# State products moved behind the outputs' products, and PReLU given to two engines in turn: a Mamba-2 scan with a two-layer PReLU network behind it

## The chip, the cores and the metric

The kernel runs on one core of one Trainium2 chip. The metric is the time of one execution on the device in microseconds. A core has TensorE (PE: matrix products, which write to the accumulation memory PSUM), VectorE (DVE), ScalarE (ACT), GpSimd (POOL) and SyncE (SP), which in this kernel issues nearly all transfers. Each engine works through its own queue in order, and engines wait for each other through semaphores.

## The reference

Everything is fp32. A state-space scan over 4 batches, 8 heads, 768 positions in chunks of 32 (the result does not depend on the chunk), head size 32, state size 16; its output is laid out as 3072 tokens of 256 features and goes through two matrix products with a PReLU between them.

```python
for c in range(nc):                       # chunks of one (batch, head)
    cum = np.cumsum(la, axis=-1)          # la = log(clip(a, 1e-6, 1))
    L = np.exp(cum[:, :, :, None] - cum[:, :, None, :]) * causal
    y_intra = np.einsum('bhij,bhjd->bhid', CB * L, xc)        # CB = C B^T
    y_inter = np.einsum('bhin,bhnd->bhid', Cc, state) * np.exp(cum)[..., None]
    state = decay_full * state + sum_j(B_j x_j * decay_from_j)
...
x = attn_out.transpose(0, 2, 1, 3).reshape(3072, 256)
h = x @ w_in                              # 256 x 2048
g = np.maximum(h, 0.0) + alpha * np.minimum(h, 0.0)
return g @ w_out                          # 2048 x 256
```

## The kernel before

**Pairs.** The scan uses chunks of 128 positions, two chunks (a *pair*) at a time: 12 pairs, three to a batch. `pair(gp)` is a generator: each `yield` ends a stage, and `ssm(gp, n)` runs the next n stages of a pair. The stages of a pair from 4 on (`fine`) are: transposes of B and C (L469) and a copy to `bc` by ScalarE (L472); four pieces of the decays by VectorE (`half_decays`, two scans each, L438), with the spread of C by ScalarE (`spread_c`, L484) at the last; the *state products* (`added`, L520: what the pair adds to the state, from x and `bn`, two chunks, or one for the pair that closes a batch), the state update (`states`, L532 by VectorE or L529 by ScalarE at a batch's first pair; the masked `sm` by GpSimd, L535) and the decayed C (`c_decayed`, GpSimd, L487); the products of B and C (`products_bc`, L570, four row groups, of which the first two go to PSUM tiles of `ss_tile()` and the last two to `spare()`) and two of the four multiplications by the decays (L606); the other two; the *outputs' products* (L622 from the state, L629 within the chunk) and the copies of their two tiles to `xT` by ScalarE (L636). `pair_loads` makes `bn` on GpSimd (L385) from the loaded B. From `early[0] = None` on (L1002), `ss_tile()` hands out two PSUM tiles in turn.

**Groups and quads.** Two pairs make a group of 512 tokens. Group 0 goes through the network by `hidden` and `output`, while the weights arrive in 16 pieces, which are converted by `convert_a` (ScalarE and GpSimd, L218 to L228) and `convert_b`/`convert` (VectorE and GpSimd). The loop over `f` (L978) runs this stage; tile f of the hidden layer gets its PReLU at L651 (ScalarE) and L652 (VectorE). The decay rows of the second two batches are loaded at f = 5 (L122, on SP's queue) and prepared by VectorE at f = 8 (L339). Groups 1 to 5 use a form with seven products instead of eight (a Strassen-Winograd scheme), in four *quads* each (z = 0 to 3, `quad(g, z, after)`): seven first-layer products, two PSUM tiles A and Y (both of the `hp` ring of two, which `spare()` shares), PReLUs, sums by GpSimd (L806, L815), and then seven second-layer products (`product`, L747), which the next quad issues between its own. The first-layer products come in the order: A; Y; A again; A with the third token sum; Y with b22; A with the fourth token sum; Y with b21. Between them ScalarE copies A out (L780, L789), VectorE adds (L791, L795), and, ahead of the last product, ScalarE copies the saved first product into Y (L801). `combine` adds up the finished group's second-layer products during the next group's first quad, with ScalarE copies at L831 and L834.

**The order of the work** is written out by hand (`manual_schedule`): every engine executes its instructions in the order in which the program issues them. `quad` calls `after(j)` for j = 1 to 14, and `after` issues there what belongs to step j: a second-layer product of the quad before (`with_gram` in quads with z even while there is a pair to come, `without` otherwise; the first has nothing at step 9), weight sums, and stages of the pairs (`steps`: which pair's next stage runs at (z, j)). A group's two pairs belong to the next group: one is worked on from z = 3 of the group before to z = 1, the other from z = 1 to z = 3. The state products stand at (0, 9) and (2, 9), between the products A with the fourth token sum and Y with b21; the outputs' products at (1, 5) and (3, 5).

**PReLU** in a quad (`prelu`, L751) is, for a tile of two halves p, o = h * (alpha * s) by ScalarE and then o = max(h * s, o) by VectorE: one operation per half, first both of ScalarE (L755), then both of VectorE (L757). Both read h from the same PSUM tile, save for the one called g22, whose h is in SBUF (`c22`).

Of the kernel before, what the change touches and what calls it, by code (L numbers as in the profile page):

```python
# [9 lines left out]
F32 = mybir.dt.float32  # L10
U32 = mybir.dt.uint32
U16 = mybir.dt.uint16
ALU = mybir.AluOpType
# [9 lines left out]
def kernel(  # L23
# [25 lines left out]
    nc = tc.nc  # L49
# [6 lines left out]
    P = 128  # L56
    Q = 128
# [268 lines left out]
    held = {}  # L326
    bns = {}

    def identity_bank():


        m5_bank.append(bank(3))
        nc.scalar.copy(out=m5_bank[0][:, HT:], in_=ident_h[:, :HT])
        ident_p.append(m5_bank[0][:, HT:])
# [77 lines left out]
    def spare():  # L412

        return ps_h.tile([P, GT], F32, name="hp", tag="hp")

    def pair(gp):

        b, c = divmod(2 * gp, CPB)
        nat, abc, xt, ap = loads["p", gp]
        last = c + 2 == CPB  # L420
        dec = work.tile([P, 2, H, Q], F32, name="dec")
        dv = dec.rearrange("p k h t -> p k (h t)")

# [37 lines left out]
            yield  # L461


        tp = spare() if gp == 1 else ss_tile()
        if gp == 0:
            keep_warm(tp, 3, Q)
# [23 lines left out]
        fine = gp >= 2 * GC // 2  # L490
        if gp < 2:
            spread_c()
        if gp == 0:
# [2 lines left out]
            dps = spare()  # L496
            keep_warm(dps, 6, Q)
            yield
        bn = bns.pop(gp) if gp in bns else pair_loads(gp)
        if gp == 1:  # L500
            c_decayed()
            dps = spare()
# [1 line left out]
        elif gp:  # L504
            yield

        nk = 1 if last else 2  # L510
        st = [masked.get(b)]
        new = work.tile([P, 2, P], F32, name="state")
        sm = work.tile([P, 2, P], F32, name="sm")

        def added(dps):
            dps = dps.rearrange("p (k m) -> p k m", m=P)
            for k in range(nk):
                for w in range(KC):
                    ws = slice(64 * w, 64 * w + 64)
                    nc.tensor.matmul(dps[ws, k], bn[:, k, ws], xt[:, k, w * P : (w + 1) * P],  # L520
                                     start=True, stop=True, tile_position=(0, 64 * w),
                                     skip_group_check=True)
            return dps

        def states(dps):
            for k in range(nk):
                old = state.get(b)
                if old is None:
                    nc.scalar.copy(out=new[:, k], in_=dps[:, k])  # L529
                else:  # L530
                    e = (k + 1) * Q - 1
                    nc.vector.scalar_tensor_tensor(out=new[:, k], in0=old, scalar=pf[:, e : e + 1],  # L532
                                                   in1=dps[:, k], op0=ALU.mult, op1=ALU.add)
                state[b] = new[:, k]
            nc.gpsimd.tensor_tensor(out=sm[:, :nk], in0=new[:, :nk],  # L535
                                    in1=hmask.unsqueeze(1).to_broadcast([P, nk, P]), op=ALU.mult)
            st.extend(sm[:, k] for k in range(nk))
            masked[b] = st[-1]

        if fine:  # L540
            for k in range(2):
                for w in range(2):
                    half_decays(k, w)
                    if k == 1 and w == 1:
                        spread_c()
                    yield
        else:
            if gp > 1:
                states(added(ss_tile()))
                c_decayed()  # L550
# [33 lines left out]
        if gp == 0:  # L584
            gram = products_bc()
            dps = added(dps)
            yield
            c_decayed()
            times(dec[:, :, :2], one_less(gram))
        elif gp == 1:  # L590
            gram = products_bc()
            g0 = one_less(gram)
            yield
            decays(1)
            states(dps)
            times(dec[:, :, :2], g0)
        else:
            if fine:
                states(added(ss_tile()))
                c_decayed()  # L600
            yield
            gram = products_bc()
        for i, r in enumerate(r for r in ((2, 3, 0, 1) if fine else (3, 2, 1, 0) if gp > 1 else range(4))
                              if r in gram):
# [6 lines left out]
        yield  # L611


        y = [ss_tile()[:, : 2 * Q].rearrange("p (k t) -> p k t", k=2) for w in range(KC)]
        if gp < 2:
            keep_warm(y[0].rearrange("p k t -> p (k t)"), 2 - gp)
        begun = False
# [7 lines left out]
        for k in range(2):  # L625
            for w in range(KC):
                for q in range(4):
                    h = 4 * w + q
                    nc.tensor.matmul(y[w][32 * q : 32 * q + 32, k], xt[:, k, h * D : (h + 1) * D],  # L629
                                     dec[:, k, h], start=False, stop=True,  # L630
                                     tile_position=(0, 32 * q), skip_group_check=True)
        g, q = divmod(2 * gp, GC)
        if q == 0:
            xts[g] = xtp.tile([P, KC, GT], F32, name="xT")
# [116 lines left out]
    def prelu(o, h, z, i, by=(nc.scalar, nc.vector)):  # L751

        fs = [slice(4 * z + 2 * p + i, 4 * z + 2 * p + i + 1) for p in range(2)]
        for p in range(2 if nc.scalar in by else 0):
            nc.scalar.mul(o[:, p], h[:, p], s_alpha[:, fs[p]])  # L755
        for p in range(2 if nc.vector in by else 0):
            nc.vector.scalar_tensor_tensor(out=o[:, p], in0=h[:, p], scalar=s_mul[:, fs[p]],  # L757
                                           in1=o[:, p], op0=ALU.mult, op1=ALU.max)

    def quad(g, z, after):  # L760

# [261 lines left out]
    for i in range(NZ * (NG - 1)):  # L1023
        g, z = divmod(NZ + i, NZ)
        nxt = 2 * g + 2

        def after(j, g=g, z=z, i=i, nxt=nxt):
            places = with_gram if nxt < NP and z % 2 == 0 else without
            if i and j in places:
                product(*divmod(NZ + i - 1, NZ), places[j])  # L1030
            if i == 0:
                for f, half in last_out.get(j, ()):
                    output(NF - LATE + f, half)
            if (i, j) in ((0, 13), (1, 2)):
# [24 lines left out]
        quad(g, z, after)  # L1059
# [31 lines left out]
```

## Time and profile before

| what | value |
|---|---|
| median of 10 runs | 374.3 us (373.64 to 374.84) |
| the profiled execution: time, span | 374.0 us, 372.1 us |
| TensorE clock granted | 0.999 |
| busy: PE, DVE, POOL, ACT | 98%, 65%, 54%, 48% of the span |
| L747 products (second layer), 128x256 | 320 and 240 records, 381 and 379 ns each |
| L772 products (first layer), 128x256 | 480 records in three groups, 379 to 390 ns each |
| L757 PReLU by VectorE | 120 on PSUM, 479 ns each |
| L755 PReLU by ScalarE | 120 on PSUM, 470 ns each |
| L815 sums by GpSimd | 58, 1269 ns each |

How to read it: the span is the stretch from the first to the last instruction in the profile, and what lies around it makes the difference to the execution's time. An fp32 product appears as two records, so that one `first` (two products) is four. A record's duration is longer than the distance to the next one, since products are pipelined: 379 ns against 216 ns from start to start. The timeline merges neighbouring instructions of a kind; its columns are the start in microseconds from the span's start, the length of the merged stretch in microseconds, the engine, the line, the operation, output <- input by the program's names, for TensorE the rows and columns of the array in use, the shape, and the count; in square brackets stands the idle time before it and what ended it. Idle time of an engine that is not the bottleneck costs nothing by itself.

### The profile page before, as it was taken

What the parts mean: (1) busy time and instruction counts of PE and PEld (TensorE: products, weight loads), DVE (VectorE), ACT (ScalarE), POOL (GpSimd) and SP (SyncE); (2) the same over time, 40 slices, a digit from 0 to 9 for tenths busy, and PEclk for the clock granted to TensorE, in tenths of its full rate; (3) what the DMA queues carried; (4) which work ended last, traced back from release to release, by engine and by line L of the source; (5) the groups of instructions that cost most, each with busy time, mean ns of one, the idle gap of its engine ahead of it and who ended that gap; (6) DMA issues with size and microseconds to landing.
All of it is one profiled execution on the core that took longest, in us unless ns stands there. A gap on an engine that the chain in (4) does not pass through costs nothing.

```text
span 372.1 us, 6183 instructions
## 1 busy us (share of the span) xinstructions
PE 365.0 (98%) x2223; PEld 294.5 (79%) x2223; DVE 243.3 (65%) x462; ACT 179.4 (48%) x384; POOL 200.7 (54%) x211
## 2 busy tenths in 40 slices
PE   8989999999999999999999999999999999999996
PEld 8766656578788888788788788788788788888884
DVE  7996889976448548748638847637848644643364
ACT  2657866435355355445444445445535525553541
POOL 4875566777929654724644625555445355264512
PEclk9999999999999999999999999999999999999999
DMA  8989998902176201005504603701901001001004
GB/s 162 201 171 342 220 289 187 194 11 58 56 129 113 71 3 56 2 0 78 136 3 66 146 2 56 158 0 31 176 8 29 2 0 25 7 0 30 1 0 85
DMA packets 121878, 30.71 MB, mean 83 GB/s; under 512 B 93736, under 2 KB 117752, under 8 KB 121848
## 3 DMA queue, kind: packets, MB, share of 16 engines
q1 hardware_dynamic: 116736, 29.74, 35.7%
q10 hardware_dynamic: 5112, 0.59, 1.1%
q8 instruction: 17, 0.28, 0.3%
q14 instruction: 13, 0.11, 0.1%
HBM read 26.98 MB, written 3.34 MB: 81 GB/s over the span
## 4 chain that ended last, share of the span: by engine, by line
PE 87%; DMA 5%; DVE 4%; SPq 2%; ACTq 1%; ACT 1%; issue 1%; POOL 0%; POOLq 0%; DVEq 0%
PE hp L772 34%; PE bank L747 32%; PE bank L686 6%; PE hp L648 4%; DMA raw<-in_moe_w_in_dram 3%; PE ss L629 3%; PE ss L570 2%; PE ss L622 1%; DVE dec L438 1%; PE ss L520 1%; DMA nat<-in_B_dram 1%; PE hp L570 1%; PE ss L469 1%; SPq L165 1%; DMA ap<-pf 1%; SPq L163 1%
## 5 line engine op out<-in xcount | busy, mean ns | idle before, releaser
L815 POOL TENSOR_TENSOR gt<-gt 128x512 f32<-128x512 f32 x58 | 73.6, 1269 | 30.7 <-DVE gt L757 23.8
L757 DVE SCALAR_TENSOR_TENSOR gt<-hp,s_mul,gt 128x256 f32<-128x256 f32 x120 | 52.5, 479 | 46.8 <-ACT gt L755 45.8
L747 PE MATMUL bank<-gt,w_out 128*128 128x256 f32 x320 | 82.4, 381 | 0.0
L755 ACT ACTIVATE gt<-hp,s_alpha 128x256 f32<-128x256 f32 x120 | 50.3, 470 | 46.7 <-PE hp L772 32.5
L747 PEld LDWEIGHTS bank<-gt,w_out 128*128 128x128 f32 x320 | 60.1, 190 | 10.4 <-issue 2.3
L806 POOL TENSOR_TENSOR gt<-gt 128x512 f32<-128x512 f32 x20 | 25.4, 1271 | 78.8 <-DVE gt L757 78.8
L747 PE MATMUL bank<-gt,ws 128*128 128x256 f32 x240 | 58.3, 379 | 0.0
L747 PEld LDWEIGHTS bank<-gt,ws 128*128 128x128 f32 x240 | 45.1, 190 | 5.8
L438 DVE TENSOR_TENSOR_SCAN dec<-abc,bank 128x256 f32<-128x256 f32 x80 | 48.1, 661 | 0.0
L772 PE MATMUL hp<-xs,w_in 128*128 128x256 f32 x160 | 42.8, 390 | 0.0
L772 PE MATMUL hp<-xT,w_in 128*128 128x256 f32 x160 | 41.9, 384 | 0.0
L772 PE MATMUL hp<-xs,ws 128*128 128x256 f32 x160 | 41.1, 379 | 0.0
L791 DVE TENSOR_TENSOR hp<-hp,u 128x512 f32<-128x512 f32 x20 | 14.0, 700 | 39.8 <-ACT u L789 39.8
L780 ACT COPY m<-hp 128x512 f32<-128x512 f32 x20 | 11.7, 586 | 51.8 <-PE hp L772 51.8
L772 PEld LDWEIGHTS hp<-xs,w_in 128*128 128x128 f32 x160 | 28.7, 189 | 7.7 <-issue 3.0
L772 PEld LDWEIGHTS hp<-xs,ws 128*128 128x128 f32 x160 | 30.4, 190 | 4.1
L772 PEld LDWEIGHTS hp<-xT,w_in 128*128 128x128 f32 x160 | 29.7, 190 | 5.0 <-issue 1.4
L686 PE MATMUL bank<-w_out,gt 128*128 128x256 f32 x128 | 31.0, 384 | 0.0
L686 PEld LDWEIGHTS bank<-w_out,gt 128*128 128x128 f32 x128 | 23.7, 190 | 6.6 <-issue 3.5
L795 DVE TENSOR_TENSOR c<-hp,m 128x512 f32<-128x512 f32 x20 | 13.6, 681 | 19.3 <-PE hp L772 19.3
L648 PE MATMUL hp<-xT,w_in 128*128 128x512 f32 x48 | 22.8, 598 | 0.9 <-DVE gt L652 0.7
L789 ACT COPY u<-hp 128x512 f32<-128x512 f32 x20 | 11.7, 585 | 22.5 <-PE hp L772 22.5
(156 smaller groups left out, 553.3 us busy)
## 6 DMA issues: line engine op xcount, KB each, us to landing
abc<-z SPq DMA_DIRECT2D x20, 512.0 KB, 5.2
raw<-in_moe_w_in_dram SPq DMA_DIRECT2D x8, 512.0 KB, 5.0
raw<-in_moe_w_out_dram SPq DMA_DIRECT2D x8, 512.0 KB, 7.3
xt<-in_x_dram SPq DMA_DIRECT2D x24, 128.0 KB, 2.8
out_dram<-o_sb SPq DMA_DIRECT2D x32, 64.0 KB, 1.9
nat<-in_B_dram SPq DMA_DIRECT2D x22, 64.0 KB, 2.8
nat<-in_C_dram SPq DMA_DIRECT2D x22, 64.0 KB, 2.6
ap<-pf SPq DMA_DIRECT2D x11, 128.0 KB
```

The lines of the kernel that those rows point to most:

```text
L438: nc.vector.tensor_tensor_scan(out=dv[:, k, hs], data0=abc[k][:, hs], data1=ident_p[0], initial=0.0, op0=ALU.mult, op1=ALU.add)
L648: nc.tensor.matmul(hp, w_in[:, k, f * P : (f + 1) * P], xts[g][:, k], start=(k == 0), stop=(k == KC - 1))
L686: nc.tensor.matmul(pos[0][t // 2][:, t % 2], gt[:, t * Q : (t + 1) * Q], w_out[:, f], start=(f == 0 and t % 2 == 0), stop=(f == NF - 1), s ...
L747: nc.tensor.matmul(ms[g][i][:, h], w, blocks[g, z][n][:, p], start=(q == 0 and h == 0), stop=(q == NQ - 1), skip_group_check=True)
L755: nc.scalar.mul(o[:, p], h[:, p], s_alpha[:, fs[p]])
L757: nc.vector.scalar_tensor_tensor(out=o[:, p], in0=h[:, p], scalar=s_mul[:, fs[p]], in1=o[:, p], op0=ALU.mult, op1=ALU.max)
L772: nc.tensor.matmul(to[:, p], w(2 * z + p), b, start=start and p == 0, stop=True, skip_group_check=True)
L780: nc.scalar.copy(out=m1, in_=A)
L791: nc.vector.tensor_tensor(out=Y, in0=Y, in1=u2, op=ALU.add)
L795: nc.vector.tensor_tensor(out=c22, in0=A, in1=m5, op=ALU.add)
L806: nc.gpsimd.tensor_tensor(out=tc_, in0=g22, in1=g12, op=ALU.subtract)
L815: eng.tensor_tensor(out=o, in0=x0, in1=x1, op=ALU.subtract)
```

## The change

It has four parts. (1) `prelu` goes through the two halves and issues ScalarE's operation and VectorE's for the first half, and then both for the second. (2) A fine pair's generator is reordered: `bn` and the state products come first, then the state update, then transposes, decays and the rest; `c_decayed` joins `spread_c`. The state products of the next pair are written into the unused second half of the outputs' second PSUM tile (`beside`), and a `yield` stands between the outputs' products and the copies to `xT`. At (1, 5) and (3, 5) the loop now issues: the outputs' products, the next pair's state products, the two copies to `xT`, and the next pair's state update. The stages at (0, 9) and (2, 9) are gone; `bn` is made there. (3) Pair 4 runs its first four stages ahead of the loop over quads (state products and update among them), with `bn` made at f = 14. (4) The first part of the conversion of weight piece 6 is issued at f = 5, behind the sixth tile's (f = 5) PReLU by ScalarE, instead of at the end of f = 4. Moved code is shown shortened:

```diff
+    beside = {}
...
         def added(dps):
-            dps = dps.rearrange("p (k m) -> p k m", m=P)
+            dps = dps[:, : 2 * Q].rearrange("p (k m) -> p k m", m=P)
...
         if fine:
+            bn = bns.pop(gp) if gp in bns else pair_loads(gp)
+            dps = added(beside.pop(gp) if gp in beside else ss_tile()[:, : 2 * Q])
+            yield
+            states(dps)
+            yield
...
         if fine:
             for k in range(2):
                 for w in range(2):
                     half_decays(k, w)
                     if k == 1 and w == 1:
                         spread_c()
+                        c_decayed()
                     yield
...
         else:
-            if fine:
-                states(added(ss_tile()))
-                c_decayed()
-            yield
+            if not fine:
+                yield
             gram = products_bc()
...
-        y = [ss_tile()[:, : 2 * Q].rearrange("p (k t) -> p k t", k=2) for w in range(KC)]
+        ys = [ss_tile() for w in range(KC)]
+        y = [t[:, : 2 * Q].rearrange("p (k t) -> p k t", k=2) for t in ys]
+        if fine:
+            beside[gp + 1] = ys[1][:, 2 * Q :]
...
+        if fine:
+            yield
         g, q = divmod(2 * gp, GC)
...
     def prelu(o, h, z, i, by=(nc.scalar, nc.vector)):
...
-        for p in range(2 if nc.scalar in by else 0):
-            nc.scalar.mul(o[:, p], h[:, p], s_alpha[:, fs[p]])
-        for p in range(2 if nc.vector in by else 0):
-            nc.vector.scalar_tensor_tensor(out=o[:, p], in0=h[:, p], scalar=s_mul[:, fs[p]],
-                                           in1=o[:, p], op0=ALU.mult, op1=ALU.max)
+        for p in range(2):
+            if nc.scalar in by:
+                nc.scalar.mul(o[:, p], h[:, p], s_alpha[:, fs[p]])
+            if nc.vector in by:
+                nc.vector.scalar_tensor_tensor(out=o[:, p], in0=h[:, p], scalar=s_mul[:, fs[p]],
+                                               in1=o[:, p], op0=ALU.mult, op1=ALU.max)
...
-        if f < FIRST + 2:
-            convert_a(*pieces[f + 1 + (f > FIRST)])
+        for i in {FIRST: (5,), FIRST + 1: (6, 7)}.get(f, ()):
+            convert_a(*pieces[i])
         convert_next(first=f > FIRST)
-        if f == FIRST:
-            convert_a(*pieces[6])
+        if f == 14:
+            bns[4] = pair_loads(4)
...
-    ssm(2 * GC // 2, 2)
+    ssm(2 * GC // 2, 4)
...
-    steps = {(0, 1): 0, (0, 2): 0, (0, 5): 0, (0, 9): 0, (0, 13): 0, (1, 1): 0, (1, 5): 0,
-             (1, 12): 1, (1, 14): 1, (2, 1): 1, (2, 2): 1, (2, 5): 1, (2, 9): 1, (2, 13): 1,
+    steps = {(0, 1): 0, (0, 2): 0, (0, 5): 0, (0, 13): 0, (1, 1): 0, (1, 5): 0,
+             (1, 12): 1, (1, 14): 1, (2, 1): 1, (2, 2): 1, (2, 5): 1, (2, 13): 1,
              (3, 1): 1, (3, 5): 1, (3, 12): 2, (3, 14): 2}
...
                 ssm(nxt + steps[z, j])
+
+                if j == 5 and z % 2:
+                    for p in (1, 0, 1):
+                        if nxt + z // 2 + p < NP:
+                            ssm(nxt + z // 2 + p)
...
-            ahead = nxt + {(1, 3): 1, (3, 8): 2}.get((z, j), NP)
+            ahead = nxt + {(0, 9): 1, (2, 9): 2}.get((z, j), NP)
```

More of the change, by code (lines that the diff above doesn't have):

```diff
@@ L420, in pair @@
         last = c + 2 == CPB
+        fine = gp >= 2 * GC // 2
         dec = work.tile([P, 2, H, Q], F32, name="dec")
@@ L461, in pair, with added, states @@
             yield
+        nk = 1 if last else 2
+        st = [masked.get(b)]
+        new = work.tile([P, 2, P], F32, name="state")
+        sm = work.tile([P, 2, P], F32, name="sm")
+        def added(dps):
+            dps = dps[:, : 2 * Q].rearrange("p (k m) -> p k m", m=P)
+            for k in range(nk):
+                for w in range(KC):
+                    ws = slice(64 * w, 64 * w + 64)
+                    nc.tensor.matmul(dps[ws, k], bn[:, k, ws], xt[:, k, w * P : (w + 1) * P],
+                                     start=True, stop=True, tile_position=(0, 64 * w),
+                                     skip_group_check=True)
+            return dps
+        def states(dps):
+            for k in range(nk):
+                old = state.get(b)
+                if old is None:
+                    nc.scalar.copy(out=new[:, k], in_=dps[:, k])
+                else:
+                    e = (k + 1) * Q - 1
+                    nc.vector.scalar_tensor_tensor(out=new[:, k], in0=old, scalar=pf[:, e : e + 1],
+                                                   in1=dps[:, k], op0=ALU.mult, op1=ALU.add)
+                state[b] = new[:, k]
+            nc.gpsimd.tensor_tensor(out=sm[:, :nk], in0=new[:, :nk],
+                                    in1=hmask.unsqueeze(1).to_broadcast([P, nk, P]), op=ALU.mult)
+            st.extend(sm[:, k] for k in range(nk))
+            masked[b] = st[-1]
+        if fine:
[4 more added lines that the diff above has]
+            yield
         tp = spare() if gp == 1 else ss_tile()
@@ L488, in c_decayed @@
                                     op=ALU.mult)
-        fine = gp >= 2 * GC // 2
         if gp < 2:
@@ L498, in pair @@
             yield
-        bn = bns.pop(gp) if gp in bns else pair_loads(gp)
+        if not fine:
+            bn = bns.pop(gp) if gp in bns else pair_loads(gp)
         if gp == 1:
@@ L505, in pair @@
             yield
[L510 to L515, printed above, removed]
-            dps = dps.rearrange("p (k m) -> p k m", m=P)
[L517 to L538, printed above, removed]
         if fine:
@@ L597, in pair @@
         else:
-            if fine:
-                states(added(ss_tile()))
-                c_decayed()
-            yield
+            if not fine:
+                yield
             gram = products_bc()
@@ L631, in pair @@
                                      tile_position=(0, 32 * q), skip_group_check=True)
+        if fine:
+            yield
         g, q = divmod(2 * gp, GC)
```

## The prediction

> **What bounds the kernel now.** I read the page first, then the chain of waits, then the timeline of TensorE, ScalarE and VectorE in one stretch of the main loop, then the list of who waited for whom.
>
> ```profile
> PE 365.0 (98%) x2223; PEld 294.5 (79%) x2223; DVE 243.3 (65%) x462; ACT 179.4 (48%) x384; POOL 200.7 (54%) x211
> PE   8989999999999999999999999999999999999996
> PE 87%; DMA 5%; DVE 4%; SPq 2%; ACTq 1%; ACT 1%; issue 1%; POOL 0%; POOLq 0%; DVEq 0%
> ```
>
> TensorE is busy in every slice and carries 87% of the chain that ended last; nobody else holds more than 5%. So a change counts in two ways only: what TensorE itself does, and whether it now has to wait. The reader should see that the second is a matter of slack on ScalarE and VectorE, whose low shares say nothing about latency. The TensorE timeline of an even quad (z = 2) with a pair in hand:
>
> ```profile
> 177.23 1.03 PE L772 MATMUL hp<-xs,w_in 128*128 128x256 f32 x4
> 178.19 0.66 PE L520 MATMUL ss<-xt,bn 128*64 128x128 f32 x8
> 178.78 1.13 PE L772 MATMUL hp<-xT,w_in 128*128 128x256 f32 x4
> 179.74 1.03 PE L747 MATMUL bank<-gt,w_out 128*128 128x256 f32 x4
> ...
> 181.58 0.71 PE L570 MATMUL hp<-cz,bc 32*128 32x256 f32 x2
> ...
> 183.83 1.03 PE L772 MATMUL hp<-xT,w_in 128*128 128x256 f32 x4
> ```
>
> One product of four records takes 0.863 us start to start (0.216 each). From 177.23 to the product of 179.74 pass 2.51 us, where two products alone would take 1.73: the state products (L520) cost 0.78 us, of which 0.09 on entering and 0.10 on leaving (the record after them lasts longer, 1.13 against 1.03). The two engines beside it:
>
> ```profile
> 175.75 0.84 ACT L755 ACTIVATE gt<-hp,s_alpha 128x256 f32<-128x256 f32 x2 [1.33 <-PE hp L772]
> 176.48 0.90 ACT L755 ACTIVATE gt<-c,s_alpha 128x256 f32<-128x256 f32 x2
> 177.59 0.59 ACT L801 COPY hp<-m 128x512 f32<-128x512 f32 x1 [0.21 <-DVE gt L757]
> 178.36 0.84 ACT L755 ACTIVATE gt<-hp,s_alpha 128x256 f32<-128x256 f32 x2 [0.17 <-PE hp L772]
> 180.00 0.84 ACT L755 ACTIVATE gt<-hp,s_alpha 128x256 f32<-128x256 f32 x2 [0.81 <-PE hp L772]
> ```
>
> ```profile
> 175.43 0.67 DVE L795 TENSOR_TENSOR c<-hp,m 128x512 f32<-128x512 f32 x1
> 176.63 0.88 DVE L757 SCALAR_TENSOR_TENSOR gt<-hp,s_mul,gt 128x256 f32<-128x256 f32 x2 [0.53 <-ACT gt L755]
> 177.42 0.87 DVE L757 SCALAR_TENSOR_TENSOR gt<-c,s_mul,gt 128x256 f32<-128x256 f32 x2
> 179.23 0.88 DVE L757 SCALAR_TENSOR_TENSOR gt<-hp,s_mul,gt 128x256 f32<-128x256 f32 x2 [0.94 <-ACT gt L755]
> 180.02 0.72 DVE L532 SCALAR_TENSOR_TENSOR state<-state,ap,ss 128x128 f32<-128x128 f32 x2
> 180.88 0.88 DVE L757 SCALAR_TENSOR_TENSOR gt<-hp,s_mul,gt 128x256 f32<-128x256 f32 x2
> ```
>
> Two things to see. A PReLU out of PSUM is two ScalarE operations and then two VectorE ones, never mixed: VectorE starts at 176.63, 0.04 after ScalarE's second ends (0.04 to 0.09 over the twenty quads). And the copy L801 ends at 178.18, while the product that adds into the same tile starts at 178.78: 0.6 us of slack, made by the state products that stand in between.
>
> **What the Trainium skill says.** "PSUM — Partial Sum Buffer", section "PSUM bank collisions raise a hardware error": two engines may not touch the same bank and quadrant at once, ScalarE and VectorE reads included, and it is for semaphores to prevent it. An hp tile (128x512 fp32) is shared by both halves of a PReLU; the trace agrees in that no L757 on hp overlaps an L755 on the same tile. The same page, "Engine vs sequencer instructions": these queues are strictly first in, first out, which is how the ScalarE lines above stand. "TensorEngine Tiling (Array Packing)", "Key Properties": a change of tiling mode drains TensorE; the trace shows 0.31 instead of 0.22 start to start into L520, and 0.32 for the first full record after it.
>
> **The change part by part.** Times are relative to T, the start of the quad's first PReLU operation on ScalarE (175.75 above).
>
> PReLU in turn. The order on each engine stays; the waits do not. With ScalarE 0, VectorE 0, ScalarE 1, VectorE 1 written in that order, ScalarE's second operation now waits for VectorE's first, because both read one hp tile. Before: 0.37 to the second start, 0.47, handoff 0.07, 0.40, 0.48 = 1.79. After: 0.47 + 0.07 + 0.48 + 0.09 + 0.47 + 0.07 + 0.48 = 2.13 (0.09 is VectorE to ScalarE, as ahead of L801). Queued behind ScalarE's waiting operation are the two multiplications of c, the copy L801 and the next PReLU.
>
> The copy: ScalarE 0 to 0.47; VectorE 0.54 to 1.02; ScalarE 1.11 to 1.58; the c operations from 1.48, 0.41 apart, to 2.39; copy 2.30 to 2.89. Before it ended at 2.43. TensorE starts 0.14 after a copy it waits for (the stalls on u2, L789), so the last first-layer product can start at 3.03.
>
> State products taken out of the even quad. With nothing between, TensorE would be ready for that product at T + 1.48 + 0.86 = 2.34. It waits until 3.03, where it stood anyway (178.78 = T + 3.03). The 0.78 us (0.57 with four records, pairs that close a batch) are not gained: the stall on L801 takes their place.
>
> What is late next. Second PReLU: ScalarE 2.80 to 3.27, VectorE 3.34 to 3.82, ScalarE 3.91 to 4.38, VectorE 4.45 to 4.93 (before 4.36). Third: ScalarE 4.28 to 4.75, VectorE 4.83 to 5.31, ScalarE 5.40 to 5.87, VectorE 5.94 to 6.42 (before 6.01). The fourth row group of L570 writes that same hp tile, and TensorE is in order behind it: before, it started at 181.81 = T + 6.06, 0.05 after VectorE; after, T + 6.47. The next quad follows 2.02 later either way. So +0.41 for this quad and the one at 233.25. The z = 2 quads with four-record state products (118.32, 290.75) reached that row group at 5.88 and 5.83: +0.6 each. In z = 0 quads VectorE's c sum ends later (+0.05), and from the second group on the copy of L834 stands between the second and third PReLU on ScalarE (+0.25): 6.80 against 6.05, 5.82 and 6.05: +0.75, +1.0, +0.75. The first quad, with a VectorE weight sum in between: +0.7. Sum over eight even quads: 2.0 + 3.2 = +5.2 us.
>
> State products put into odd quads, behind L629. Entering from the outputs' mode 0.20, own 0.385 (0.167 with four), leaving 0.20 where L629 left with 0.20 before: 0.59 or 0.37. Odd quads' TensorE has no slack to absorb them: 4 x 0.59 + 3 x 0.37 = +3.5. Pair 4's go ahead of the loop, 0.09 + 0.385 + 0.20 + 0.05 = +0.7. In odd quads the copy (T + 2.88) stays ahead of its product (T + 3.2), so no stall there; the third PReLU ends 0.4 later, under the 6.66 to 7.10 at which the next quad's second tile is wanted.
>
> What moves with them. The second xT copy waits for the state products (same PSUM tile), and state updates (0.34 each) for that copy: they end about T − 0.75, ahead of the c sum; cover is the product running meanwhile. bn (0.64 on GpSimd) moves into even quads behind L806; the loads it needs are issued by 175.44, with 2.8 median to land 178.2, and L806 ends at 179.71. If that cover fails, only products due eight steps later wait. sm and cd stand earlier, covered by GpSimd's idle time; ahead of the loop bn delays the first token sum 0.64, to 82.6, wanted at 83.4. SP's order is unchanged. The end: the last PReLU is 0.4 late and its first product waits for it (it starts as VectorE ends, 361.55): +0.3; the quad before with L834, +0.1.
>
> The conversion. The sixth tile's ScalarE operation starts at 36.4 instead of 37.53. VectorE's chain gains about 0.95, and TensorE's stall at 47.58 (a gap of 1.04) goes. But VectorE waits from 53.38 to 54.09 for the rows' load, whose place is unchanged, and runs without a gap to 69.23, where TensorE waits for it (69.28). The gain is given back: −0.1, bounds 0 and −0.9.
>
> Sum: 5.2 + 3.5 + 0.7 + 0.4 − 0.1 = +9.7. On the profiled execution, 374.0 us in all with a span of 372.1: 383.7. The median of the runs is 0.3 higher: 384.0.
>
> **The rivals.** (1) *It gets faster.* If ScalarE's slack covered the mixed order, the seven moved blocks would save one entry and exit each, 7 x 0.2 = 1.4, with up to 0.9 from the conversion: 372.5. It decides where the copy ends at T + 2.2; I have 2.89, and even the old order has 2.43. Chance 0.06. (2) *Only the copy's stall.* If the fourth row group of L570 did not wait for the third PReLU, the even quads would lose about 0.1 each: 0.8 + 3.5 + 0.7 + 0.3 = 5.3, giving 379.5. Against it: it started 0.05 behind VectorE in three quads I looked at. Chance 0.12. (3) *The loads too.* If bn waits 1 us or more for its load, VectorE and GpSimd fall behind, and handoffs nearer 0.15 than 0.08 add 0.3 per PReLU chain: +14 to +17, 390. Chance 0.08.
>
> **How the numbers follow.** The case above 0.72, the rivals 0.06, 0.12, 0.08; the remaining 0.02 is no change. Likeliest 384.0, its own range 381.5 to 387 (0.05 on each of some six handoffs in eight quads is 2.4, the conversion 0.9). The range for 8 in 10 reaches into case 2: 378.5 to 388.5. Faster 0.06, same 0.02, slower 0.92; 0.2% is about what a measurement of this kernel can tell from no change.
>
> **What would show it.** Right: TensorE idle ahead of the last first-layer product in even quads, put down to ScalarE's copy, and ahead of L570's hp rows; ScalarE and VectorE alternating in the timeline, 2.1 us a PReLU; even quads about 0.4 to 1.0 longer, odd ones 0.6. Wrong: two ScalarE operations back to back, or the even quads shorter by 0.8.

## The result, and the profile after

The kernel after takes 381.67 us (median of 8 runs, 381.39 to 382.42), the kernel before in the same comparison 374.33: a ratio of 1.020, 95% interval 1.0187 to 1.0213. The profiled execution took 381.91 us with a span of 380.0 us at a granted clock of 0.999, so nothing of the 7.9 us between the two spans is the clock's.

The same three lines of the page as before: busy time by engine, TensorE's row of the slices, the chain of waits by engine.

```profile
PE 369.2 (97%) x2223; PEld 295.3 (78%) x2223; DVE 250.1 (66%) x462; ACT 182.0 (48%) x384; POOL 201.1 (53%) x211
...
PE   8989999999999999999999999999999999999996
...
PE 80%; DVE 8%; ACT 7%; SPq 2%; issue 1%; DMA 1%; POOL 0%; POOLq 0%; ACTq 0%
```

Busy shares and slices hardly move: PE is at 97% and the slices are the same digit for digit. What moves is the chain: TensorE's share falls from 87% to 80%, and VectorE and ScalarE, with 5% together before, now hold 15%. A quad's PReLUs are called by their tiles: g12 is the first, g21 the second, g11 the third; the fourth, g22, has its h in SBUF and is never in turn, in any kernel here. The even quad (z = 2) that was shown of before stands here with T = 179.80, the start of its first PReLU on ScalarE. Lines are numbered anew: the products L772 and L747 are now L786 and L760, the row groups L570 are L580, PReLU's L755 and L757 are L769 and L771. TensorE's timeline, from the product with the fourth token sum on:

```profile
181.27 1.03 PE L786 MATMUL hp<-xs,w_in 128*128 128x256 f32 x4
182.63 1.13 PE L786 MATMUL hp<-xT,w_in 128*128 128x256 f32 x4 [0.33 <-ACT hp L815]
183.59 1.03 PE L760 MATMUL bank<-gt,w_out 128*128 128x256 f32 x4
...
186.01 0.67 PE L580 MATMUL hp<-cz,bc 32*128 32x256 f32 x2
...
188.01 0.81 PE L786 MATMUL hp<-xT,w_in 128*128 128x256 f32 x3
```

The state products are gone from between the first two lines, and instead TensorE waits for ScalarE's copy (L815, which was L801). A bracket counts idle time from the modelled end of the record before; from start to start it is 1.36 us where a product takes 0.86, so 0.50 of the 0.78 us is lost again here. ScalarE and VectorE in the same quad:

```profile
179.80 0.47 ACT L769 ACTIVATE gt<-hp,s_alpha 128x256 f32<-128x256 f32 x1 [1.33 <-PE hp L786]
180.82 0.47 ACT L769 ACTIVATE gt<-hp,s_alpha 128x256 f32<-128x256 f32 x1 [0.55 <-DVE gt L771]
181.19 0.89 ACT L769 ACTIVATE gt<-c,s_alpha 128x256 f32<-128x256 f32 x2
181.99 0.58 ACT L815 COPY hp<-m 128x512 f32<-128x512 f32 x1
```

```profile
180.30 0.48 DVE L771 SCALAR_TENSOR_TENSOR gt<-hp,s_mul,gt 128x256 f32<-128x256 f32 x1 [0.16 <-ACT gt L769]
181.33 0.48 DVE L771 SCALAR_TENSOR_TENSOR gt<-hp,s_mul,gt 128x256 f32<-128x256 f32 x1 [0.54 <-ACT gt L769]
181.73 0.87 DVE L771 SCALAR_TENSOR_TENSOR gt<-c,s_mul,gt 128x256 f32<-128x256 f32 x2
...
185.45 0.48 DVE L771 SCALAR_TENSOR_TENSOR gt<-hp,s_mul,gt 128x256 f32<-128x256 f32 x1 [0.54 <-ACT gt L769]
```

Each engine now waits about 0.55 us for the other inside a PReLU out of PSUM. ScalarE's operation ends at 180.27, VectorE's starts at 180.30; VectorE's ends at 180.78, ScalarE's next starts at 180.82. So a PReLU takes 2.01 us (179.80 to 181.81) where it took 1.76 in the quad shown of before (175.75 to 177.51), the copy ends at T + 2.77 (before 2.43), and the third PReLU at T + 6.13 (before 6.00). What keeps the two engines apart could be the `hp` tile in PSUM, which both read, or the `gt` tile in SBUF, which both write. The lines at g22, where the two share a `gt` tile alone, speak for the first: VectorE begins its first half at 181.73, while ScalarE works on the second until 182.08. They overlap so, by 0.33 to 0.36 us, in each of the twenty quads of this trace, and never on an `hp` tile.

The difference by place, from the starts of the quads' first products in the two traces: eight even quads +0.37, 1.07, 0.45, 0.13, 0.67, 0.14, 0.45, 0.36 = +3.64; seven odd ones +0.37, 0.47, 0.60, 0.37, 0.58, 0.58, 0.37 = +3.34; pair 4 ahead of the loop +0.72; the end +0.2: 7.9 in all. The medians lie 7.3 us apart. (This execution began the first group 0.74 us later than that of before, 31.37 against 30.63, and lost 0.74 less at the tile of 47.58; the two cancel here, and experiments 3 take them apart.)

### The profile page after: what moved, and what is told of

Its sections match the earlier page's. It is cut to its first block, busy times and chain, and to the rows that moved or that the text cites. A ratio compares the mean times of both kernels' runs of the same rounds, so it can differ in the third digit from the quotient of the medians.

```text
span 380.0 us, 6122 instructions
## 1 busy us (share of the span) xinstructions
PE 369.2 (97%) x2223; PEld 295.3 (78%) x2223; DVE 250.1 (66%) x462; ACT 182.0 (48%) x384; POOL 201.1 (53%) x211
## 3 DMA queue, kind: packets, MB, share of 16 engines
HBM read 26.98 MB, written 3.34 MB: 80 GB/s over the span
## 4 chain that ended last, share of the span: by engine, by line
PE 80%; DVE 8%; ACT 7%; SPq 2%; issue 1%; DMA 1%; POOL 0%; POOLq 0%; ACTq 0%
PE hp L786 28%; PE bank L760 26%; PE bank L699 7%; PE hp L661 6%; ACT gt L769 5%; DVE gt L771 4%; PE ss L640 2%; PE hp L580 2%; PE ss L633 1%; PE ss L478 1%; PE ss L511 1%; PE hp L676 1%; DVE dec L435 1%; DVE dec L441 1%; SPq L163 1%
## 5 line engine op out<-in xcount | busy, mean ns | idle before, releaser
L771 DVE SCALAR_TENSOR_TENSOR gt<-hp,s_mul,gt 128x256 f32<-128x256 f32 x120 | 57.7, 483 | 50.7 <-ACT gt L769 49.5
L769 ACT ACTIVATE gt<-hp,s_alpha 128x256 f32<-128x256 f32 x120 | 56.3, 473 | 65.2 <-DVE gt L771 34.7
L760 PE MATMUL bank<-gt,w_out 128*128 128x256 f32 x320 | 82.6, 382 | 0.0
L760 PEld LDWEIGHTS bank<-gt,w_out 128*128 128x128 f32 x320 | 60.1, 190 | 10.6 <-issue 2.3
L760 PE MATMUL bank<-gt,ws 128*128 128x256 f32 x240 | 58.3, 379 | 0.0
L760 PEld LDWEIGHTS bank<-gt,ws 128*128 128x128 f32 x240 | 45.1, 190 | 5.8
L786 PE MATMUL hp<-xT,w_in 128*128 128x256 f32 x160 | 41.9, 384 | 2.6 <-ACT hp L815 2.6
L786 PE MATMUL hp<-xs,w_in 128*128 128x256 f32 x160 | 42.8, 390 | 0.0
L786 PE MATMUL hp<-xs,ws 128*128 128x256 f32 x160 | 41.1, 379 | 0.0
L786 PEld LDWEIGHTS hp<-xT,w_in 128*128 128x128 f32 x160 | 29.7, 190 | 9.4 <-ACT hp L815 5.8
L786 PEld LDWEIGHTS hp<-xs,w_in 128*128 128x128 f32 x160 | 28.7, 189 | 7.5 <-ACT u L803 1.3
L786 PEld LDWEIGHTS hp<-xs,ws 128*128 128x128 f32 x160 | 30.4, 190 | 4.1
L493 POOL TENSOR_TENSOR sm<-state,bmask 128x256 f32<-128x256 f32 (+1 forms) x12 | 7.9, 660 | 34.3 <-DVE state L490 34.1
```

Of the source, the lines that this page charges most:

```text
L760: nc.tensor.matmul(ms[g][i][:, h], w, blocks[g, z][n][:, p], start=(q == 0 and h == 0), stop=(q == NQ - 1), skip_group_check=True)
L786: nc.tensor.matmul(to[:, p], w(2 * z + p), b, start=start and p == 0, stop=True, skip_group_check=True)
```

## Experiments 1: PReLU in turn, the moves, and both

Six kernels were made from the kernels before and after by taking PReLU or parts of it into the old order or the new one. "In turn" is the order of the kernel after (ScalarE, VectorE, ScalarE, VectorE), the old order that of the kernel before (both of ScalarE, then both of VectorE). Four of them, with the kernels before and after, show every part with and without the other; the numbers first, then each one's edit and expectation:

| kernel | in turn | moves | median, us | ratio to before (95%) |
|---|---|---|---|---|
| before | – | – | 374.3 to 374.6 | 1 |
| e1 | – | yes | 374.59 | 1.0010 (0.9993 to 1.0027) |
| e2 | all | – | 380.51 | 1.0160 (1.0131 to 1.0190) |
| e3 | first only | yes | 377.39 | 1.0071 (1.0049 to 1.0093) |
| e4 | second, third | yes | 380.73 | 1.0165 (1.0142 to 1.0188) |
| after | all | yes | 381.67 | 1.0200 (1.0187 to 1.0213) |

"Moves" includes the conversion's new order here. Each ratio is to the kernel before in the same comparison; e2, e3 and e4 have 4 runs each, e1 has 12 and the kernel after 8.

**e1**, the kernel after with the old PReLU:

```diff
-        for p in range(2):
-            if nc.scalar in by:
-                nc.scalar.mul(...)
-            if nc.vector in by:
-                nc.vector.scalar_tensor_tensor(...)
+        for p in range(2 if nc.scalar in by else 0):
+            nc.scalar.mul(...)
+        for p in range(2 if nc.vector in by else 0):
+            nc.vector.scalar_tensor_tensor(...)
```

> The kernel after, with PReLU as in the kernel before: both ScalarE operations, then both VectorE operations. The moves and the conversion's order stay. My theory (the loss is what the two parts make together: in turn, the copy of m1 and the third PReLU come later, and the state products no longer cover them): a PReLU takes about 1.79 us again, the copy ends near T + 2.4, TensorE waits some 0.1 us for it, the even quads come out 0.35 to 0.57 us shorter than in the kernel before, the odd ones 0.37 to 0.59 longer as in the kernel after (+3.34 in all) and pair 4 ahead of the loop costs +0.72: 374.5 us, within 1 us of the kernel before. Rival (the moves alone cost it: more changes of tiling mode, loads and copies beside): it stays at 380 to 382.

Measured 374.59, as expected. The even quads are 0.48 to 0.54 us shorter than before in four of the five from which eight records moved away (0.28 in the first), 0.27 to 0.38 in the other three; the odd ones are longer by what was moved there. The moves by themselves cost nothing that shows, as long as the conversion's order comes with them (experiments 3).

**e2**, the kernel before with only `prelu` changed (the diff above, the other way round).

> The kernel before, with only PReLU in turn. My theory: the copy ends near T + 2.8, still ahead of its product, which the state products hold until T + 3.03, so no stall there; the third PReLU ends some 0.2 us later and the fourth row group behind it with it, so +0.2 to 0.3 for each of eight even quads, +0.2 at the end: 375.8 to 376.8 us. Rival (the order in turn costs all of it by itself): 380 to 382. Rival (the order in turn is free, since ScalarE and VectorE have slack): 374.3.

Measured 380.51: the expectation failed, and the rival that the order in turn costs nearly everything by itself held. No stall on the copy is listed in its trace, as expected; where four records stand in front of the product, it comes at most 0.10 us later than before. The groups of TensorE's instructions of this kernel (columns: busy time and mean, then idle time before and what ended it) put the loss elsewhere:

```profile
L773 PE MATMUL hp<-xT,w_in 128*128 128x256 f32 x160 | 41.9, 385 | 0.0
...
L570 PE MATMUL hp<-cz,bc 32*128 32x256 f32 x72 | 16.7, 412 | 2.4 <-DVE gt L758 2.2
```

The row groups of L570 wait for VectorE's PReLU. Why it is that late is in VectorE's timeline of the same kind of quad (T = 178.26):

```profile
182.49 0.48 DVE L758 SCALAR_TENSOR_TENSOR gt<-hp,s_mul,gt 128x256 f32<-128x256 f32 x1 [0.54 <-ACT gt L756]
182.89 0.72 DVE L532 SCALAR_TENSOR_TENSOR state<-state,ap,ss 128x128 f32<-128x128 f32 x2
183.53 0.48 DVE L758 SCALAR_TENSOR_TENSOR gt<-hp,s_mul,gt 128x256 f32<-128x256 f32 x1
184.55 0.48 DVE L758 SCALAR_TENSOR_TENSOR gt<-hp,s_mul,gt 128x256 f32<-128x256 f32 x1 [0.54 <-ACT gt L756]
```

In this arrangement the state updates (L532) stand on VectorE between the second and the third PReLU. The second, in turn, ends later, the updates behind it too, and the third PReLU's first VectorE operation starts at T + 5.27. In the old order ScalarE has both halves done by then, and VectorE would need 0.40 + 0.48 from there; in turn, ScalarE's second operation waits for it and is itself waited for: 0.48 + 0.03 + 0.47 + 0.04 + 0.48. It ends at T + 6.77 instead of 6.00. My expectation had left the updates out.

**e3 and e4**, the kernel after with parts in the old order; e3 is

```diff
-        prelu(g21, A, z, 1)
+        prelu(g21, A, z, 1, (nc.scalar,))
+        prelu(g21, A, z, 1, (nc.vector,))
...
-        prelu(g11, Y, z, 0)
+        prelu(g11, Y, z, 0, (nc.scalar,))
+        prelu(g11, Y, z, 0, (nc.vector,))
```

and e4 the same for g12 alone.

> The kernel after, with only the first PReLU of a quad (g12) in turn; g21 and g11 in the old order. My theory: the copy behind g12 ends at T + 2.77 as in the kernel after, so TensorE's stall on it (about 0.45 us in each even quad) stays, but the third PReLU ends near T + 5.8 and the fourth row group is not late: even quads about 0.2 us shorter than before, odd ones +3.34, entry +0.72, so 375.5 to 377 us. Rival (only the copy's stall sets the even quads): it stays at 381 to 382.

> The kernel after, with the first PReLU of a quad (g12) in the old order and g21 and g11 in turn. My theory: the copy ends near T + 2.4 and TensorE's stall on it shrinks to about 0.1 us, but the chain of the second and third PReLU goes on in turn and ends near T + 6.0, some 0.13 us ahead of the kernel after: about 1 us faster than the kernel after, 380 to 381. Rival (the copy's stall is what costs): the even quads gain 0.35 us each, 378 to 379, or nearer to the kernel before.

e3 measured 377.39, a little above its range and far from the rival; e4 380.73, inside its range. The first PReLU in turn costs 2.8 us over e1, the other two 6.1, both together 7.1: less than the sum. The groups of TensorE's instructions of e3:

```profile
L786 PE MATMUL hp<-xT,w_in 128*128 128x256 f32 x160 | 41.9, 385 | 2.6 <-ACT hp L815 2.6
...
L580 PE MATMUL hp<-cz,bc 32*128 32x256 f32 x72 | 13.4, 402 | 0.0
```

and of e4:

```profile
L786 PE MATMUL hp<-xT,w_in 128*128 128x256 f32 x160 | 41.9, 385 | 0.1
...
L580 PE MATMUL hp<-cz,bc 32*128 32x256 f32 x72 | 16.8, 412 | 2.9 <-DVE gt L771 2.5
```

and of the kernel after:

```profile
L786 PE MATMUL hp<-xT,w_in 128*128 128x256 f32 x160 | 41.9, 384 | 2.6 <-ACT hp L815 2.6
...
L580 PE MATMUL hp<-cz,bc 32*128 32x256 f32 x72 | 16.4, 412 | 1.4 <-DVE gt L771 1.1
```

In e3 all of the wait is at the copy, in e4 nearly all at the row groups, in the kernel after there is some at both. e4 took the copy's wait of the kernel after away and got 1 us for it, since most of that came back one wait later.

**e8 and e9** ask the same of the kernel before: e8 has the first and the second PReLU in turn, e9 only the third.

> The kernel before, with only the first and the second PReLU of a quad (g12, g21) in turn; the third (g11) in the old order. My new theory (in the kernel before with all in turn, 380.5, it is the third PReLU: behind VectorE's two state updates its three last operations run one after the other, and the fourth row group waits for them): the third PReLU ends near T + 6.15 instead of 6.0, so +0.15 for an even quad, perhaps 1 at the first: 375.5 to 377. Rival (each PReLU in turn costs about a third of the 5.9 us): 378 to 379.

> The kernel before, with only the third PReLU (g11) in turn. My new theory: VectorE reaches its first operation at T + 5.1, behind the state updates as before; then 0.48 + 0.04 + 0.47 + 0.04 + 0.48 to T + 6.63, where the old order ends at 6.0: the fourth row group 0.63 us late in each of eight even quads, +0.2 at the end: 378.5 to 380. Rival (each PReLU a third): 376 to 376.7.

e8 measured 375.99 (ratio 1.0035, 1.0022 to 1.0048), inside its range. e9 measured 377.78 (1.0083, 1.0050 to 1.0116): the third PReLU is the dearest, but 3.3 us is less than the 4 to 5.5 that I expected. I had VectorE reach its first operation at T + 5.1; it starts at 4.76 to 4.98 in the quads with eight records of state products, since in turn it needs ScalarE's first half only, so the third PReLU ends at T + 6.27 to 6.48 and not at 6.63 (the first quad aside, where it starts at 5.49). So in the kernel before it was ScalarE's second half that VectorE waited for, and not the state updates. The two add up to 4.8 of the 5.9 us of e2. Where the rest comes from shows in the seventh quad: the second PReLU in turn pushes the updates, and with them VectorE's start on the third from T + 4.91 (e9) to 5.27 (e2).

## Experiments 2: does covering the copy help?

**e7**, the kernel after with one second-layer product moved to where the state products stood, between the last two first-layer products of an even quad:

```diff
-    with_gram = {3: 1, 5: 2, 7: 3, 8: 5, 11: 7, 13: 6, 14: 4}
+    with_gram = {3: 1, 5: 2, 7: 3, 8: 5, 9: 7, 13: 6, 14: 4}
```

> The kernel after, with one product of four records put between the last two first-layer products of an even quad, where the state products stood before (it is taken from behind the last one). My theory (the chain of three PReLUs in turn on ScalarE and VectorE sets the even quads, and a stall that is filled comes back behind it): TensorE no longer waits for the copy, but the last first-layer product comes about 0.35 us later, the third PReLU's end with it, and the wait at the fourth row group grows from 0.1 to 0.25 into 0.6 to 0.8 us: 1 to 3 us slower than the kernel after, 382.7 to 384.5. Rival (the uncovered copy is what costs, so covering it pays): the 0.45 us of each even quad come back, 378 us.

Measured 382.44 (ratio 1.0216, 1.0197 to 1.0235), 0.8 us above the kernel after, whose ratio of 1.0200 (1.0187 to 1.0213) has an interval that overlaps: just under my range, 4 us from the rival, and at any rate not faster. The groups of TensorE's instructions:

```profile
L786 PE MATMUL hp<-xT,w_in 128*128 128x256 f32 x160 | 41.2, 380 | 0.3 <-ACT hp L815 0.3
...
L580 PE MATMUL hp<-cz,bc 32*128 32x256 f32 x72 | 16.8, 412 | 5.6 <-DVE gt L771 5.6
```

The wait for the copy shrinks from 2.6 to 0.3 us, and the wait for the third PReLU grows from 1.1 to 5.6. What sets an even quad shows when the kernels are laid side by side: in each of the last six even quads that have a pair in hand, the fourth row group of `products_bc` starts 0.05 to 0.06 us behind the third PReLU's end, and the next quad's first product 2.02 to 2.03 behind that. Times from T, for a quad with z = 0 (the fifth) and one with z = 2 (the seventh):

| kernel | third PReLU ends | fourth row group | next quad's first product |
|---|---|---|---|
| before | 6.00, 6.00 | 6.05, 6.05 | 8.07, 8.08 |
| e1 | 5.51, 5.46 | 5.57, 5.51 | 7.59, 7.53 |
| e3 | 5.87, 5.81 | 5.93, 5.87 | 7.95, 7.89 |
| e4 | 6.28, 6.04 | 6.33, 6.09 | 8.36, 8.11 |
| after | 6.45, 6.13 | 6.50, 6.19 | 8.53, 8.21 |
| e7 | 6.44, 6.34 | 6.50, 6.40 | 8.52, 8.42 |
| e2 | 6.62, 6.77 | 6.67, 6.83 | 8.70, 8.85 |

So VectorE's end of the third PReLU sets the even quad in all of them, the kernel before included, where the wait is too short for any view to list it: the fourth row group starts there at 181.808, 0.23 us behind the third, and 0.007 behind it where nothing holds it (at 43.874, in the first group). What sets that end differs. With the second and third PReLU in the old order (before, e1, e3) it lies 2.97 to 2.98 us behind the start of the product with b21: there TensorE's order of work decides, and taking the state products away from in front of that product pays. In e8, where the second is in turn and only the third is not, it lies 2.99 to 3.33 us behind. With the third in turn it lies 3.1 to 3.8 us behind. In e7 that is only the longer PReLU itself; in the kernel after, e2 and e4 the PReLUs ahead are late too, and the place of the product hardly matters: it starts at T + 2.83 in the kernel after and at 2.48 in e4 (z = 2), and the PReLU ends at 6.13 and 6.04; with z = 0 it starts at 2.90 in the kernel after and at 3.20 in e7, and the PReLU ends at 6.45 and 6.44.

## Experiments 3: the conversion

**e5** is the kernel after, **e10** the kernel e1, each with the conversion's order of before; **e6** is the kernel before with that of after. e6:

```diff
-        if f < FIRST + 2:
-            convert_a(*pieces[f + 1 + (f > FIRST)])
+        for i in {FIRST: (5,), FIRST + 1: (6, 7)}.get(f, ()):
+            convert_a(*pieces[i])
         convert_next(first=f > FIRST)
-        if f == FIRST:
-            convert_a(*pieces[6])
```

> The kernel after, with the conversion in the order of the kernel before (one piece's first part behind the sixth tile, the seventh's behind the seventh). My theory (the earlier conversion is given back where VectorE waits for the rows' load): TensorE's stall of about 1 us near 47.6 is back, VectorE's wait for the rows near 53 to 54 shrinks by as much, the tile near 69.3 starts where it did, and the time is that of the kernel after, 381.7, within 0.3 us. Rival (the conversion's gain is kept, and the rest of the change costs that much more): up to 0.9 us slower than the kernel after.

> The kernel before, with only the conversion's order changed. My theory: the same as before within 0.3 us (374.3 to 374.6), with the stall of 1.04 us near 47.6 gone and VectorE's wait for the rows longer by as much. Rival (the gain is kept): 373.5 to 373.8. Rival (it is the seventh piece that now comes late): 0.5 us slower or more.

e6 measured 374.03 against 374.44 (ratio 0.9989, 0.9981 to 0.9997), 0.1 us beyond my theory's "within 0.3". e5 measured 382.70 (1.0221, 1.0206 to 1.0237), 1.0 us above the kernel after by the medians and 0.8 by the two ratios: my theory that the gain is given back failed there. ScalarE's timeline of the kernel before and of e5, and then TensorE's of e5:

```profile
36.37 0.68 ACT L218 ACTIVATE wt<-raw 128x512 f32<-128x512 f32 x1 [0.98 <-DMA raw<-in_moe_w_in_dram]
```

```profile
37.19 0.69 ACT L218 ACTIVATE wt<-raw 128x512 f32<-128x512 f32 x1 [1.75 <-DMA raw<-in_moe_w_in_dram]
...
38.32 0.69 ACT L664 ACTIVATE gt<-hp,s_alpha 128x512 f32<-128x512 f32 x1
```

```profile
48.41 1.96 PE L661 MATMUL hp<-xT,w_in 128*128 128x512 f32 x4 [1.15 <-DVE gt L665]
```

The seventh piece's first operation stands ahead of the sixth tile's PReLU on ScalarE, in a queue that is strictly first in, first out (the Trainium skill, "PSUM — Partial Sum Buffer", section "Engine vs sequencer instructions"), and waits for the piece's load: 1.75 us here, 0.98 in the kernel before. The PReLU is late by that and the operations' own time, and ten us later TensorE stands. With the new order the PReLU comes first and the load has landed when its turn comes (in the traces of the kernel after, e1, e6 and e11 no wait for it is listed). How long the wait is differs from execution to execution: in the traces of the other kernels with the old order it is 0 in e2, e8 and e12 and 0.84 in e9, and TensorE's stand goes with it. The moves change nothing that is issued ahead of f = 14, so the longer wait in e5 is not theirs. That gave a new theory, which e10 tests:

> The kernel after with PReLU as before (the kernel that measured 374.6), and the conversion's order of before too. New theory (ahead of the sixth tile's PReLU on ScalarE stands an operation that waits for the seventh piece's load; moved behind, it frees 0.7 to 1.2 us at 47.6, of which only a part is lost again to VectorE's wait for the rows): 0.4 to 1.0 us slower, 375.0 to 375.6. Rival (the gain is given back in full where the rest is not in turn): 374.6, within 0.2.

e10 measured 375.55 (ratio 1.0028, 1.0017 to 1.0039), 1.0 us above e1 by the medians and 0.7 by the ratios, with 1.66 us of waiting for the load and the same 1.15 us ahead of the tile. The new theory held. So the conversion's order is worth 0.7 to 1.0 us beside the moves, each of the two comparisons by ratios being good to about 0.75, and 0.4 (0.1 to 0.7) in the kernel before; that it is worth more beside the moves is not shown. The moves alone, without it, cost about 1.0 us (375.55 against 374.50).

Where some of the gain goes in the kernel before shows in VectorE's timeline of e6:

```profile
54.54 0.62 DVE L339 TENSOR_SCALAR r<-rows 96x128 f32<-96x128 f32 x1 [1.51 <-DMA rows<-in_a_dram]
```

VectorE, earlier now, waits 1.51 us for the rows' load (0.72 before), and TensorE stands 0.31 us longer at the tile of 69.25. In e11 and e12 the rows' load is issued ahead of the fourth pair's loads, in e11 on top of e6, in e12 on the kernel before:

```diff
+        if f == 5:
+            load_rows(1)
         if f in (5, 10):
             load_pair(3 + f // 10)
-        if f == 5:
-            load_rows(1)
```

> The kernel before, with the conversion's order of the change and the rows' load issued ahead of the fourth pair's loads (at about 36.5 us instead of 48.1). My theory (what the earlier conversion wins at 47.6 is partly lost again because VectorE waits 1.5 us for the rows near 54, which is seen at the tile of 69.25, where TensorE stands 0.33 us): that wait and that stand are gone, 373.5 to 373.9, about 0.3 us faster than with the conversion's order alone (374.0) and 0.4 to 1.0 faster than before. Rival (the rows are no limit, or the pair's loads, now 0.5 us later, are): 374.0 or slower.

> The kernel before, with only the rows' load issued ahead of the fourth pair's loads. My theory: VectorE's wait of 0.72 us for the rows goes, but with the conversion's old order TensorE has lost its time at 47.6 already and does not stand at 69.3: the same as before within 0.3 us (374.2 to 374.6). Rival (the rows' load is what counts): 373.5 to 374.

e11 measured 373.52 against 374.61 (ratio 0.9972, 0.9965 to 0.9980): faster than the kernels before and after. VectorE no longer waits:

```profile
52.73 0.22 DVE L339 TENSOR_SCALAR r<-rows 96x128 f32<-96x128 f32 x1
```

e12 measured 374.03 (0.9989, 0.9978 to 0.9999), 0.6 below its comparison's 374.61 (0.4 by the ratio) and below the 374.2 to 374.6 that I expected. In its profiled execution the sixth tile's PReLU did not wait for the seventh piece at all, so that execution cannot tell the rows' own part from a load that landed earlier. That stays open. Nor do the medians show that the rows count only after the earlier conversion: their load moved ahead is worth 0.5 us on top of e6 (373.52 against 374.03) and 0.6 without it, or 0.6 and 0.4 by the ratios.

## Why the prediction was right, and where its sum was off

It forecast 384.0 us (378.5 to 388.5) and slower; it is 381.67. That is inside the range, and at the lower end of the likeliest case's own (381.5 to 387). The sum of +9.7 stands against +7.9 in the profile; the other 0.5 of the 2.3 us is that the prediction put the median 0.3 us above the profiled execution, where the kernel after has it 0.24 below.

**PReLU in turn.** The mechanism is as predicted: ScalarE's second operation waits for VectorE's first. The Trainium skill ("PSUM — Partial Sum Buffer", section "PSUM bank collisions raise a hardware error") has two engines kept apart on one bank and quadrant, reads included; in all twenty quads of the trace L769 and L771 never overlap on one hp tile, and they do at g22, whose h is in SBUF. The size was off: 2.13 us predicted, 2.01 measured. I took handoffs (from the end of one engine's operation to the start of the other's that waits for it) of 0.07 and 0.09 us; they are 0.03 to 0.04. The 1.79 that I had for the old order was too long by the same: it takes 1.75 to 1.80.

**The copy.** Predicted end at T + 2.89 and TensorE's start at 3.03; measured 2.77 and 2.83. The 0.14 from a copy to TensorE was taken from another stall and is 0.05 to 0.06 here. The stall is there and is put down to ScalarE's copy, as the prediction said it would be.

**Even quads.** Predicted +5.2, measured +3.64: the same sizes once more, now over three PReLUs (the fourth row group at T + 6.47 predicted and 6.19 measured for z = 2; 6.80 and 6.50 for z = 0). This is most of the error. Quad by quad the sequence holds, z = 0 worse than z = 2, except for the second of them (+1.07 against 0.6): there the third PReLU ends at T + 6.89, with ScalarE's second operation of the PReLU before it 0.64 us late, because one of VectorE's operations on g22 ahead of it lasts 1.49 us instead of 0.48. GpSimd works on a weight sum (L728) at that time; whether that is the reason no run tests. The two z = 2 quads with eight records come out 0.13 and 0.14 us longer, less than the 0.4 that was named as a sign.

**Odd quads, pair 4, end.** Predicted +3.5, +0.7 and +0.4; measured +3.34, +0.72 and +0.2. The entries and exits of the tiling modes, 0.20 us each, priced from the trace of before, carried over.

**The conversion.** Predicted −0.1, with −0.9 as the far bound; e5 and e10 show −0.7 to −1.0. The step that failed is "The gain is given back". It was read from one execution in which VectorE waited for the rows. What I had not priced is that the old order's loss depends on when the seventh piece lands, which differs between executions: from no wait at all (e2, e8, e12) over 0.98 us in the trace of before to 1.75 (e5). One trace of before could not show that spread.

**What the sum hid.** The prediction wrote "The 0.78 us are not gained: the stall on L801 takes their place", which reads as if the state products had been a cover that was lost. The arithmetic is right, the reading is not: in turn alone costs 5.9 us with the cover in place (e2), and a new cover gains nothing (e7). The three PReLUs of an even quad, one behind the other on ScalarE and VectorE, are the chain that sets it; the stall on the copy is a link of that chain and not a price beside it. Rival (2), only the copy's stall (379.5), falls with e4 and e7. Rival (1), a faster kernel, needed the copy at T + 2.2, which no kernel here reaches. Rival (3), late loads, did not show: in the trace of the kernel after `bn` (L387) waits for no load, the handoffs are shorter and not longer, and the odd and even quads add up without it.

## What to carry to other kernels

Where two engines worked on one PSUM tile here, giving them its halves in turn did not make a pipeline: it made four steps in a row (2.01 us) out of two pairs that overlap within an engine (1.75 to 1.80), and every delay ahead was then followed by the whole row. The one PReLU with its input in SBUF did overlap, so look first at what the two engines share. Before covering a stall, ask what comes next on the same chain: a table of "last input ready, consumer starts" over several kernels shows the true bound, even where TensorE is never listed as waiting. An operation that waits for a load is best queued behind whatever does not need it; here that was worth 0.4 to 1.0 us.

## What the runs showed that I had not expected

The kernel before has no idle time of TensorE listed at L570 among its groups, and yet its even quads start their fourth row group 0.05 us behind VectorE, as all the slower kernels do. A handoff between ScalarE and VectorE within a PReLU takes 0.03 to 0.04 us, half of what I had read from other places. And the same load, waited for by the same operation, ended the wait at 36.37 us in the trace of before, at 37.19 and 37.29 in e5 and e10, and in e2 and e12 it had landed when that operation's turn came at 36.18 and 36.29.
